# Row DFT by sums and differences of the half rows, and z1 units moved into the row-DFT stage

## The chip, the cores and the metric

The kernel runs on one core of a Trainium2 chip. The metric is the device time of one execution in microseconds. Before the change the median of three runs is 530.57 us (530.54 to 532.73). The core has TensorE (PE; its weight loads are shown apart as PEld), VectorE (DVE), ScalarE (ACT), GpSimd (POOL) and SyncE (SP, which here only issues DMAs).

## The reference

The input x has 2048 rows of 576 numbers in bfloat16. Its rows are normalised, and the result goes two ways: through a spectral filter (a two-dimensional real FFT, a product with complex weights, and back), and through a gated network whose second half is mixed over the rows by a 2048 x 2048 matrix.

```
xn  = layernorm(x)                                  # rows of 576
s   = irfft2(rfft2(xn) * (A_w_r + 1j*A_w_i))        # 2048 x 289 frequencies
z   = gelu(xn @ B_w_in)                             # 576 -> 4608
z1  = z[:, :2304];  z2 = layernorm(z[:, 2304:])
g   = B_w_sp @ z2 + B_b_sp                          # mixes the 2048 rows
out = x + s * silu((z1 * g) @ B_w_out)
```

## The kernel before

The row index is cut into 16 tiles of 128 rows, the 576 columns into four blocks of 128 and a tail of 64 (`KS` = 5 blocks, the last filled up with zeros). Transforms are matrix products with constant matrices. The stages, with the times at which TensorE is in them:

- **Row DFT** (13.64 to 39.59 us, after a start with warm-up matmuls and the first two tiles). For each tile m: `ln1` makes mean and variance on DVE (L234, L235) and 1/sqrt on POOL (L223, L225, a power); for the first two tiles ACT and DVE do it. `xpose` normalises on DVE (L250), transposes the five blocks on TensorE (L254), and ACT copies the result to `xnT` (L255), which stays on chip for everything that follows. `p0` multiplies the five blocks by the cosine and sine columns (L263, ten matmuls of 289 columns), ACT evicts both results (L266), and POOL issues the DMA that writes them to `Ad` in DRAM (L267).
- **Column DFT** p1 (L281, from 51.61), p2 with the filter's weights and p3 (78.03 to 132.85), **inverse** p4 and p5 (L331, L346; 132.85 to 175.66). Between them the data go through DRAM (`Ad`, `Bd`, `Ed`), and p5 writes s to `Yd` (L354).
- **Units of z2 and z1**, which fill the waits of the stages above. A z2 unit (`z2`, 96 of them) is one row tile by 384 columns: five matmuls (L370), a gelu on ACT (L374 or L380) into `Z2`, which stays on chip; sums for its normalisation are made by ACT for seven of the tiles (L377) and by DVE for the others, and a finished row tile is normalised in place on DVE. A z1 unit (`z1`, 72 of them) is 128 columns of z1 by 512 rows: five matmuls (L434) and a gelu (L437) into one of two buffers of 128 x 2048; after the fourth unit of a column tile ACT's queue writes the buffer to `Z1d` in DRAM (L439), 18 writes of 512 KB. w_in for z1 comes in groups of three column tiles (`load_win1`, two buffers).
- **Slabs.** After p5, SP issues twelve transposing DMAs of w_sp (`load_slabs`, L415). `fill(32)` and a last `fill` put what is left of z2 and z1 beside them, `slab_sums` prepares sums of the slabs on DVE.
- **Main products** (228.87 to the end at 529.2): w_sp times z2 in a scheme of seven products (`main`, L480), and the output product (`outm`, L524).

`fill(n, kinds=...)` takes the next n units; "2" means z2, "1" z1, "21" by turns; where one kind has run out, the other is taken. The order on SP, PE and DVE is the order of the program's text; on ACT and POOL the framework's scheduler sets it. All PSUM tiles of transposes, z1 and z2 come from one pool of four buffers (`psh`), those of p0 to p5 from a pool of two (`psa`). DMAs that SP and ACT issue are given one of eight completion semaphores in turn, in the order of the schedule; a DMA waits, on its issuing engine, for the DMA that held that semaphore before, and instructions behind it on that engine wait with it.

The order of the row-DFT stage is written by hand:

```
for m in range(2, MT):
    if m + 2 < MT:
        ln1([m + 2])
    if m + 1 < MT:
        xpose(m + 1)
    p0(m)
    if m >= 9:
        fill(1, norm=False)
```

Of the kernel before, what the change touches and what calls it, by code (L numbers as in the profile page):

```python
# [26 lines left out]

def build_consts(S, D, L, LC0):
    tp = 2.0 * np.pi
    KS = (D + P - 1) // P  # L30
    d = np.arange(KS * P)[:, None]
    l = np.arange(L)[None, :]
    ang = tp * ((d * l) % D) / D
    cd = np.stack([np.cos(ang), -np.sin(ang)], axis=1)
    cd[D:] = 0.0
    cd = cd.reshape(KS, P, 2 * L).transpose(1, 0, 2).reshape(P, KS * 2 * L)

    s1 = np.arange(N1)
    k1 = np.arange(N1)
    lo, hi = k1 // N2, k1 % N2  # L40
    pos = [4 * hi + 2 * c + lo for c in range(2)]
    g1 = np.zeros((N2, P, P))
    g4 = np.zeros((N2, P, P))
    for s2 in range(N2):
        th = -tp * (((s1[:, None] * k1[None, :]) % N1) / N1 + s2 * k1[None, :] / S)
        co, si = np.cos(th), np.sin(th)
        for c, c2, v in ((0, 0, co), (1, 0, -si), (0, 1, si), (1, 1, co)):
            g1[s2, c * N1 + s1[:, None], pos[c2][None, :]] = v
        cot, sit = co.T, -si.T
        for c, c2, v in ((0, 0, cot), (1, 0, -sit), (0, 1, sit), (1, 1, cot)):  # L50
            g4[s2, pos[c][:, None], c2 * N1 + s1[None, :]] = v
    m2 = np.zeros((P, P))
    m3 = np.zeros((P, P))
    a = np.arange(N2)
    th = -tp * ((a[:, None] * a[None, :]) % N2) / N2
    co, si = np.cos(th), np.sin(th)
    for lo_ in range(2):
        for c, c2, v in ((0, 0, co), (1, 0, -si), (0, 1, si), (1, 1, co)):
            m2[c * N1 + lo_ * N2 + a[:, None], c2 * N1 + 2 * a[None, :] + lo_] = v
        for c, c2, v in ((0, 0, co), (1, 0, si), (0, 1, -si), (1, 1, co)):  # L60
            m3[c * N1 + 2 * a[:, None] + lo_, c2 * N1 + lo_ * N2 + a[None, :]] = v
    m3j = np.concatenate([m3[N1:], -m3[:N1]], axis=0)
    mm = np.stack([m2, m3, m3j], axis=1).reshape(P, 3 * P)

    ceso = np.zeros((P, len(LC0), 2, L))
    dd = np.arange(L)[None, :]
    seen = 0
    for i, l0 in enumerate(LC0):
        lv = (l0 + np.arange(P))[:, None]
        th = tp * ((lv * dd) % D) / D  # L70
        cl = np.where((lv == 0) | (lv == D // 2), 1.0, 2.0) * (lv >= seen) * 0.5 / (S * D)
        ceso[:, i, 0, :] = cl * np.cos(th)
        ceso[:, i, 1, :] = -cl * np.sin(th)
        seen = l0 + P
    return dict(cdsd=cd, g1=g1.transpose(1, 0, 2).reshape(P, N2 * P), g4=g4.transpose(1, 0, 2).reshape(P, N2 * P),
                mm=mm, ceso=ceso.reshape(P, -1))
# [3 lines left out]
def kernel(  # L80
# [64 lines left out]
    nc.gpsimd.memset(mhalf[:], -0.5)  # L145

    sizes = dict(A0=12288, G4=N2 * P, CESO=NLC * 2 * L, MM=3 * P, STG=6 * L, TT=8 * L,
                 AIN=4 * 8 * L, BES=2 * 8 * L, RW=KS * Fh, XT=MT * KS * P, XN=2048, ZT=2048, WI=2 * KS * WG * P)
    offs, o_ = {}, 0
    for k_, v_ in sizes.items():  # L150
        offs[k_] = o_
# [3 lines left out]
    def reg(name, off, n):  # L155
        return AR[:, offs[name] + off: offs[name] + off + n]

    CDSD = reg("A0", 0, KS * 2 * L).rearrange("p (k c l) -> p k c l", k=KS, c=2)
    G1 = reg("A0", KS * 2 * L, N2 * P).rearrange("p (s k) -> p s k", s=N2)
    wo = KS * 2 * L + N2 * P  # L160
    WCH = [reg("A0", wo + i * 8 * L, 8 * L).rearrange("p (c h l) -> p c h l", c=2, h=4) for i in range(2)]
# [3 lines left out]
    MM = reg("MM", 0, 3 * P).rearrange("p (a k) -> p a k", a=3)  # L165
    XN = [reg("XN", i * KS * P, KS * P) for i in range(3)]
    STG = [reg("STG", i * 2 * L, 2 * L) for i in range(3)]
    PST = [reg("BES", i * 2 * L, 2 * L) for i in range(8)]
    AIN = [reg("AIN", i * 8 * L, 8 * L) for i in range(4)]
    TT = [reg("TT", i * 4 * L, 4 * L).rearrange("p (c h l) -> p c h l", c=2, h=2) for i in range(2)]  # L170
    BES = [reg("BES", i * 8 * L, 8 * L) for i in range(2)]
    WIN1 = [reg("WI", i * KS * WG * P, KS * WG * P).rearrange("p (k f) -> p k f", k=KS) for i in range(2)]
    WIN2 = reg("RW", 0, KS * Fh).rearrange("p (k f) -> p k f", k=KS)
    xnT = reg("XT", 0, MT * KS * P).rearrange("p (m k t) -> p m k t", m=MT, k=KS)
    Z1S = [reg(n_, 0, S) for n_ in ("XN", "ZT")]

    SL = reg("A0", 0, 7 * HM * NT).rearrange("p (b s t) -> p b s t", b=7, s=HM)
    ro = [offs["AIN"]]
# [21 lines left out]
    def load_x(c):  # L200
        t = AIN[c][:, 0:4 * D].rearrange("p (m d) -> p m d", m=4)
        if c == 0:
            for i in range(4):
                nc.sync.dma_start(out=t[:, i, :], in_=xv[:, i, :])
                if i == 0:
                    nc.sync.dma_start(out=CDSD, in_=cd_cdsd.ap().rearrange("p (k c l) -> p k c l", k=KS, c=2))
        else:
            nc.sync.dma_start(out=t, in_=xv[:, 4 * c:4 * c + 4, :])
        return t

    wv = B_w_in[0:(KS - 1) * P, :].rearrange("(k p) f -> p k f", p=P)
    XC = [load_x(c) for c in range(4)]
    nc.gpsimd.memset(WIN2[KT:P, KS - 1, :], 0.0)
    for g in range(2):
        sl = slice(g * Fh // 2, (g + 1) * Fh // 2)
        gl = slice(Fh + g * Fh // 2, Fh + (g + 1) * Fh // 2)
        nc.sync.dma_start(out=WIN2[:, 0:KS - 1, sl], in_=wv[:, :, gl])
        nc.sync.dma_start(out=WIN2[0:KT, KS - 1, sl], in_=B_w_in[(KS - 1) * P:D, gl])
    nc.sync.dma_start(out=G1, in_=cd_g1.ap().rearrange("p (s k) -> p s k", s=N2))

    def rstd_of(mv, n, tag):
# [25 lines left out]
    def xpose(m):  # L247
        xn = XN[m % 3]
        mean, rs = ln1_of[m]
        nc.vector.tensor_scalar(out=xn[:, 0:D], in0=XC[m // 4][:, m % 4, :], scalar1=mean, scalar2=rs,  # L250
                                op0=ALU.subtract, op1=ALU.mult)
        pt = psh.tile([P, KS, P], BF16, tag="h")
        for ks in range(KS):
            nc.tensor.transpose(pt[:, ks, :], xn[:, ks * P:(ks + 1) * P], ident[:])  # L254
        nc.scalar.activation(out=xnT[:, m, :, :], in_=pt[:], func=ACT.Identity)  # L255

    Adw = Ad[:].rearrange("(c m p) l -> m p c l", c=2, p=P)

    def p0(m):
        pa = psa.tile([P, 2, 512], F32, tag="a")  # L260
        for ks in range(KS):
            for c in range(2):
                nc.tensor.matmul(pa[:, c, 0:L], lhsT=xnT[:, m, ks, :], rhs=CDSD[:, ks, c, :],  # L263
                                 start=(ks == 0), stop=(ks == KS - 1))
        sg = PST[m % 8].rearrange("p (c l) -> p c l", c=2)
        nc.scalar.activation(out=sg, in_=pa[:, :, 0:L], func=ACT.Identity)  # L266
        nc.gpsimd.dma_start(out=Adw[m], in_=sg)  # L267

    rowv = lambda t: t[:].rearrange("(p s) l -> p (s l)", s=N2)
    colv = lambda t: t[:].rearrange("(h p) l -> p h l", p=P)  # L270
# [155 lines left out]

    SA = dict(P1=0, P2=1, P5=2, P4=3, P6=4, P7=5, P3=6)

    def z1(k):
        fi, tq = k // 4, k % 4  # L430
        wb = WIN1[(fi // WG) % 2]
        ph = psh.tile([P, 512], F32, tag="h")
        for ks in range(KS):
            nc.tensor.matmul(ph[:].rearrange("p (a t) -> p a t", a=4), lhsT=wb[:, ks, (fi % WG) * P:(fi % WG + 1) * P],  # L434
                             rhs=xnT[:, 4 * tq:4 * tq + 4, ks, :], start=(ks == 0), stop=(ks == KS - 1))
        zs = Z1S[fi % 2]
        nc.scalar.activation(out=zs[:, tq * 512:(tq + 1) * 512], in_=ph[:], func=ACT.Gelu_apprx_tanh)  # L437
        if tq == 3:
            nc.scalar.dma_start(out=Z1d[fi * P:(fi + 1) * P, :], in_=zs)  # L439
            if fi % WG == WG - 1 and fi // WG + 2 < FT // WG:  # L440
                load_win1(fi // WG + 2)

    Z1v = Z1d[:].rearrange("(f p) (h t) -> p f h t", p=P, h=2)

# [89 lines left out]
    def it_of(m):  # L534
        return (m % HM) * P // NT

    def load_win1(g):
        fs = slice((g % (FT // WG)) * WG * P, (g % (FT // WG) + 1) * WG * P)
        wb = WIN1[g % 2]
        nc.sync.dma_start(out=wb[:, 0:KS - 1, :], in_=wv[:, :, fs])  # L540
        nc.sync.dma_start(out=wb[0:KT, KS - 1, :], in_=B_w_in[(KS - 1) * P:D, fs])

    units = [(it, p) for it in range(len(ITS)) for p in range(NP)]
    zq = iter(range(MT * NZC))
    yq = iter(range(FT * 4))
# [21 lines left out]
    with tc.manual_schedule(engines={SP, PE, DVE}):  # L567
# [4 lines left out]
        ln1([0])  # L572
        xpose(0)
        nc.sync.dma_start(out=MM, in_=cd_mm.ap().rearrange("p (a k) -> p a k", a=3))
        p0(0)
        ln1([1])
        xpose(1)
        ln1([2])
        p0(1)
        ln1([3])  # L580
        xpose(2)
        for m in range(2, MT):
            if m + 2 < MT:
                ln1([m + 2])
            if m + 1 < MT:
                xpose(m + 1)
            p0(m)
            if m == 2:
                nc.scalar.activation(out=scr[:], in_=ln1_of[3][0], func=ACT.Gelu_apprx_tanh)
            if m >= 9:  # L590
                fill(1, norm=False)
    with tc.manual_schedule(engines={SP, PE, DVE}):
        for ch in range(4):
            p1_read(ch)
        load_w(0)
        load_w(1)
        for i in range(2):
            nc.gpsimd.memset(WIN1[i][KT:P, KS - 1, :], 0.0)
            load_win1(i)
        fill(14)  # L600
        for s2 in range(0, N2, 2):
            p1(s2)
# [12 lines left out]
            p3(hh)  # L615
        for ch in range(4):
            p4_read(ch)
        fill(12, kinds="21")
        for u in range(4 * NLC):
            p4(u)  # L620
            fill(1, kinds="21"[u % 2])
        for j in range(MT):
            p5(j)
            fill(1, kinds="21"[j % 2])
        load_slabs(0)
        fill(32, kinds="21")
        assert z2_done[0] == MT * NZC - 1
        nc.sync.dma_start(out=BB, in_=B_b_sp.rearrange("(a s) -> a s", a=1).to_broadcast((P, S)))
        load_z1(0)
# [53 lines left out]
```

## Time and profile before

The profiled execution took 530.98 us, of which the profile's span covers 529.2.

| stage | from, to (us) | length | PE busy | DVE | ACT | POOL | DMA share |
|---|---|---|---|---|---|---|---|
| start, warm-up | 0 to 13.64 | 13.64 | 8.57 | 7.55 | 6.78 | 6.46 | 0.90 |
| row DFT | to 39.59 | 25.95 | 25.95 | 14.66 | 21.62 | 18.19 | 0.58 |
| 14 z2 units | to 51.61 | 12.02 | 12.02 | 5.66 | 10.47 | 3.45 | 0.60 |
| p1 and units | to 78.03 | 26.42 | 24.12 | 20.21 | 22.84 | 4.13 | 0.67 |
| p2, p3 and units | to 132.85 | 54.82 | 54.15 | 34.07 | 37.40 | 4.87 | 0.82 |
| p4, p5 and units | to 175.66 | 42.81 | 42.81 | 24.95 | 29.51 | 2.06 | 0.42 |
| slab loads, units | to 228.87 | 53.21 | 52.28 | 23.32 | 28.19 | 7.07 | 0.85 |
| main products, output | to 529.20 | 300.33 | 291.03 | 215.13 | 23.67 | 125.58 | 0.32 |

How to read the profile's lines: a line of the groups names source line, engine, operation, output and inputs by the program's names (AR is the one large buffer that most tiles are parts of, ph, pa, pb and pm are PSUM), the shapes, the count; then busy time and the mean of one in ns; then the idle time of the engine just before them and what ended most of it. A timeline line begins with start and duration. A line of the waits says which instruction waited for which, how long in total, how often, and the longest. A line of stages has from:to, its length, and the busy time and number of instructions of PE, PEld, DVE, ACT and POOL, then granted TensorE clock, DMA share and GB/s.

### The profile page before, as it was taken

The numbers are of one execution on the slowest core, as the hardware profiler recorded it, in microseconds if no ns is written. First come the engines' busy times: TensorE is split into PE (matmuls) and PEld (weight loads), VectorE is DVE, ScalarE is ACT, GpSimd is POOL, SyncE is SP. The second block draws the span as 40 slices with busy tenths as digits, with TensorE's granted clock in tenths as the row PEclk, the third lists the DMA queues.
The fourth block names the chain that finished last, engine by engine and source line by source line (L and its number), as shares of the span: only waits on it lengthen the run. The fifth ranks groups of instructions, "written<-read, shape, count | busy, mean of one in ns | idle before, by whom it ended". The sixth has DMA issues, their size and how long they took to land.

```text
span 529.2 us, 9153 instructions
## 1 busy us (share of the span) xinstructions
PE 510.9 (97%) x3516; PEld 335.2 (63%) x3516; DVE 345.6 (65%) x660; ACT 180.5 (34%) x380; POOL 171.8 (32%) x230
## 2 busy tenths in 40 slices
PE   6999899999999999999999999999999999999997
PEld 3876555555666544456666677756666677788775
DVE  5925867863456635437777765986867638899944
ACT  5788887686875555420000001100000011000001
POOL 4852210001000002124434323534444234655510
PEclk9999999999999999999999999999999999999999
DMA  8926769875524799482111199312121942211102
GB/s 316 288 81 227 222 189 332 226 214 186 173 80 131 172 192 243 181 301 70 31 55 36 44 185 202 96 37 60 31 59 31 152 129 88 65 33 38 42 6 86
DMA packets 80444, 70.50 MB, mean 133 GB/s; under 512 B 38288, under 2 KB 70800, under 8 KB 80144
## 3 DMA queue, kind: packets, MB, share of 16 engines
q1 hardware_dynamic: 74784, 51.59, 37.7%
q0 software_dynamic: 2880, 8.86, 5.7%
q10 hardware_dynamic: 2736, 9.47, 4.8%
q8 instruction: 27, 0.44, 0.4%
q14 instruction: 17, 0.14, 0.1%
HBM read 40.25 MB, written 21.26 MB: 116 GB/s over the span
## 4 chain that ended last, share of the span: by engine, by line
PE 75%; DVE 9%; DMA 6%; issue 5%; ACT 2%; SPq 2%; POOL 1%; DVEq 0%; ACTq 0%; POOLq 0%
PE pm L480 33%; PE po L524 11%; PE ph L434 10%; PE ph L370 10%; DVE AR L484 4%; PE pa L263 3%; DMA AR<-in_B_w_sp_dram 3%; PE pa L346 2%; DVE AR L489 2%; SPq L415 2%; PE pb L317 2%; DMA Z1d<-AR 1%; DMA AR<-Bd 1%; PE pa L331 1%; DMA AR<-in_A_x_dram 1%
## 5 line engine op out<-in xcount | busy, mean ns | idle before, releaser
L480 PE MATMUL pm<-AR,Z_74 128*128 128x384 bf16 (+1 forms) x864 | 138.7, 308 | 0.0
L484 DVE TENSOR_TENSOR AR<-pm,AR 128x384 f32<-128x384 f32 (+3 forms) x162 | 82.3, 508 | 58.0 <-POOL AR L493 33.3
L480 PE MATMUL pm<-AR 128*128 128x384 bf16 (+1 forms) x648 | 107.0, 308 | 5.5 <-DVE AR L484 5.5
L480 PEld LDWEIGHTS <-Z_74 128*128 128x128 bf16 x864 | 84.5, 98 | 40.6
L370 PE MATMUL ph<-AR 128*128 128x384 bf16 x480 | 90.1, 326 | 0.5 <-ACT Z_74 L380 0.5
L480 PEld LDWEIGHTS <-AR 128*128 128x128 bf16 x648 | 63.3, 98 | 37.4 <-DVE AR L466 4.0
L434 PE MATMUL ph<-AR 128*128 128x512 bf16 x360 | 86.2, 379 | 0.5 <-ACT AR L437 0.5
L492 ACT ACTIVATE AR<-pm 128x384 f32<-128x384 f32 (+1 forms) x27 | 12.3, 456 | 191.3 <-PE pm L480 191.3
L468 POOL TENSOR_TENSOR AR<-Z_74,AR 128x1024 bf16<-128x1024 bf16 x27 | 57.7, 2139 | 43.0 <-PE pm L480 32.9
L524 PE MATMUL po<-AR 128*128 128x288 bf16 x540 | 66.6, 286 | 0.0
L524 PEld LDWEIGHTS <-AR 128*128 128x128 bf16 x594 | 56.9, 98 | 13.9
L370 PEld LDWEIGHTS <-AR 128*128 128x128 bf16 x480 | 46.7, 98 | 29.4 <-issue 0.7
L489 DVE TENSOR_TENSOR AR<-AR 128x384 bf16<-128x384 bf16 (+1 forms) x108 | 57.9, 536 | 3.7
L434 PEld LDWEIGHTS <-AR 128*128 128x128 bf16 x360 | 34.9, 98 | 35.2 <-issue 0.8
L437 ACT ACTIVATE AR<-ph 128x512 bf16<-128x512 f32 x72 | 42.3, 596 | 35.6 <-PE ph L434 31.4
L493 POOL TENSOR_TENSOR AR<-AR 128x384 f32<-128x384 f32 (+1 forms) x27 | 23.6, 873 | 88.9 <-ACT AR L492 88.9
L223 POOL TENSOR_SCALAR ve<-mv 128x1 f32<-128x1 f32 x30 | 5.8, 195 | 94.6 <-DVE mv L398 86.5
L527 ACT ACTIVATE TH<-po 128x576 f32<-128x576 f32 x15 | 9.8, 651 | 78.5 <-PE po L524 78.5
L380 ACT ACTIVATE Z_74<-ph 128x384 bf16<-128x384 f32 x54 | 26.1, 491 | 14.0 <-PE ph L370 10.5
L528 DVE SCALAR_TENSOR_TENSOR AR<-TH,po 128x576 bf16<-128x576 f32 x15 | 11.3, 752 | 29.9 <-ACT TH L527 29.9
L307 DVE TENSOR_TENSOR AR<-pa,AR 128x578 bf16<-128x578 f32 x32 | 22.8, 754 | 10.7 <-PE pa L305 8.7
L512 POOL DMA_DIRECT2D AR<-Yd x16 | 8.7, 547 | 55.8 <-DVE AR L529 52.7
(98 smaller groups left out, 507.9 us busy)
## 6 DMA issues: line engine op xcount, KB each, us to landing
Z1d<-AR ACTq DMA_DIRECT2D x18, 512.0 KB, 4.4
AR<-Z1d SPq DMA_DIRECT2D x36, 192.0 KB, 3.0
AR<-in_B_w_out_dram SPq DMA_DIRECT2D x1, 2592.0 KB, 11.2
Ad<-AR POOLq DMA_DIRECT2D x16, 144.5 KB, 4.1
AR<-Ad SPq DMA_DIRECT2D x4, 578.0 KB, 5.7
AR<-in_A_w_r_dram SPq DMA_DIRECT2D x16, 144.5 KB, 4.6
AR<-in_A_w_i_dram SPq DMA_DIRECT2D x16, 144.5 KB, 4.0
Bd<-AR SPq DMA_DIRECT2D x4, 578.0 KB, 2.8
```

The source lines that it names most:

```text
L263: nc.tensor.matmul(pa[:, c, 0:L], lhsT=xnT[:, m, ks, :], rhs=CDSD[:, ks, c, :], start=(ks == 0), stop=(ks == KS - 1))
L307: nc.vector.tensor_tensor(out=tt[:, c, :, :], in0=pa[:, :, 0:L], in1=wt[:, c, hh % 4:hh % 4 + 2, :], op=ALU.mult)
L370: nc.tensor.matmul(ph[:], lhsT=xnT[:, m, ks, :], rhs=WIN2[:, ks, n * ZC:(n + 1) * ZC], start=(ks == 0), stop=(ks == KS - 1))
L380: nc.scalar.activation(out=zc, in_=ph[:], func=ACT.Gelu_apprx_tanh)
L434: nc.tensor.matmul(ph[:].rearrange("p (a t) -> p a t", a=4), lhsT=wb[:, ks, (fi % WG) * P:(fi % WG + 1) * P], rhs=xnT[:, 4 * tq:4 * tq + 4 ...
L437: nc.scalar.activation(out=zs[:, tq * 512:(tq + 1) * 512], in_=ph[:], func=ACT.Gelu_apprx_tanh)
L468: nc.gpsimd.tensor_tensor(out=t, in0=zblk(p, 1, 0), in1=t2, op=ALU.subtract)
L480: nc.tensor.matmul(dst, lhsT=z[:, s, :], rhs=SL[:, SA[name], s, 0:nt], start=(s == 0 and not more), stop=(s == HM - 1), skip_group_check=more)
L484: nc.vector.tensor_tensor(out=out, in0=x, in1=y, op=ALU.add)
L489: nc.vector.tensor_tensor(out=o, in0=o, in1=zb[:, f, h, 0:nt], op=ALU.mult)
L493: nc.gpsimd.tensor_tensor(out=p1a, in0=p1, in1=B[0], op=ALU.add)
L524: nc.tensor.matmul(pv[:, hh, :], lhsT=U[:, fi, h, i * P:(i + 1) * P], rhs=WOUT[:, fi, c0 + hh * H2:c0 + hh * H2 + w // nh], start=(fi == 0 ...
```

## The change

The DFT of a row of 576 is split by the parity of the frequency. With a and b the first and the second 288 columns, even frequencies need only a + b and odd ones only a - b, with the same cosine and sine columns. `xpose` now writes the normalised row so that blocks 0 and 1 of the two halves lie by turns (in two instructions, 512 and 64 columns), and the transposed blocks are added and subtracted on DVE by a new `p0_fold`. The tails of the two halves, 32 columns each, share the fifth block, which is not folded. `p0` has six matmuls of 290 columns for ten of 289, the constant is 445 KB for 740, and ACT's eviction puts even and odd frequencies back in order with a stride of two. The rows of w_in are loaded in the same order as the blocks (`load_win`, four DMAs in place of two), and its first group for z1 is loaded ahead of the part for z2.

The order changes too. In the row-DFT loop `ln1([m + 2])` comes after `xpose(m + 1)`. Units fill that loop from m = 3 on, ten of z1 and three of z2 (before: seven of z2 from m = 9 on). The units beside p4 and p5 are z2 alone (before: by turns), and after p5 only z1 is left. z1 units go by group, then by quarter of the rows, then by column tile; each writes its own 128 KB (72 writes), from four buffers for the first sixteen units and eight after that.

```diff
-    CDSD = reg("A0", 0, KS * 2 * L).rearrange("p (k c l) -> p k c l", k=KS, c=2)
+    LE = L - L // 2
+    CDSD = reg("A0", 0, 12 * LE).rearrange("p (a k l) -> p a k l", a=2, k=3)
+    FS = [reg("G4", i * 4 * P, 4 * P).rearrange("p (a b t) -> p a b t", a=2, b=2) for i in range(4)]
...
-    Z1S = [reg(n_, 0, S) for n_ in ("XN", "ZT")]
+    Z1S = [reg("ZT", i * 512, 512) for i in range(4)]
...
+    wv = [B_w_in[a * H2:a * H2 + 2 * P, :].rearrange("(b p) f -> p b f", p=P) for a in range(2)]
+    HT = H2 - 2 * P
+
+    def load_win(t, fs):
+        for a in range(2):
+            nc.sync.dma_start(out=t[:, a:KS - 1:2, :], in_=wv[a][:, :, fs])
+            nc.sync.dma_start(out=t[a * HT:(a + 1) * HT, KS - 1, :], in_=B_w_in[a * H2 + 2 * P:(a + 1) * H2, fs])
...
+    load_win1(0)
...
-        nc.sync.dma_start(out=WIN2[:, 0:KS - 1, sl], in_=wv[:, :, gl])
-        nc.sync.dma_start(out=WIN2[0:KT, KS - 1, sl], in_=B_w_in[(KS - 1) * P:D, gl])
+        load_win(WIN2[:, :, sl], gl)
+    load_win1(1)
...
-        nc.vector.tensor_scalar(out=xn[:, 0:D], in0=XC[m // 4][:, m % 4, :], scalar1=mean, scalar2=rs,
+        xr = XC[m // 4][:, m % 4, :].rearrange("p (a d) -> p a d", a=2)
+        nc.vector.tensor_scalar(out=xn[:, 0:4 * P].rearrange("p (b a i) -> p a b i", b=2, a=2),
+                                in0=xr[:, :, 0:2 * P].rearrange("p a (b i) -> p a b i", b=2), scalar1=mean, scalar2=rs,
                                 op0=ALU.subtract, op1=ALU.mult)
+        nc.vector.tensor_scalar(out=xn[:, 4 * P:D].rearrange("p (a i) -> p a i", a=2), in0=xr[:, :, 2 * P:H2],
+                                scalar1=mean, scalar2=rs, op0=ALU.subtract, op1=ALU.mult)
...
+    def p0_fold(m):
+        xe, xo = xnT[:, m, 0:KS - 1:2, :], xnT[:, m, 1:KS - 1:2, :]
+        nc.vector.tensor_tensor(out=FS[m % 4][:, 0, :, :], in0=xe, in1=xo, op=ALU.add)
+        nc.vector.tensor_tensor(out=FS[m % 4][:, 1, :, :], in0=xe, in1=xo, op=ALU.subtract)
...
-        for ks in range(KS):
-            for c in range(2):
-                nc.tensor.matmul(pa[:, c, 0:L], lhsT=xnT[:, m, ks, :], rhs=CDSD[:, ks, c, :],
-                                 start=(ks == 0), stop=(ks == KS - 1))
+        for par in range(2):
+            for k in range(3):
+                lhs = FS[m % 4][:, par, k, :] if k < 2 else xnT[:, m, KS - 1, :]
+                nc.tensor.matmul(pa[:, par, 0:2 * LE], lhsT=lhs, rhs=CDSD[:, par, k, :], start=(k == 0), stop=(k == 2))
         sg = PST[m % 8].rearrange("p (c l) -> p c l", c=2)
-        nc.scalar.activation(out=sg, in_=pa[:, :, 0:L], func=ACT.Identity)
-        nc.gpsimd.dma_start(out=Adw[m], in_=sg)
+        nc.scalar.activation(out=sg.rearrange("p c (l a) -> p a c l", a=2),
+                             in_=pa[:, :, 0:2 * LE].rearrange("p a (c l) -> p a c l", c=2), func=ACT.Identity)
+        nc.gpsimd.dma_start(out=Adw[m], in_=sg[:, :, 0:L])
...
+    z1_order = [(WG * g + i, tq) for g in range(FT // WG) for tq in range(4) for i in range(WG)]
...
-        fi, tq = k // 4, k % 4
+        fi, tq = z1_order[k]
...
-        zs = Z1S[fi % 2]
-        nc.scalar.activation(out=zs[:, tq * 512:(tq + 1) * 512], in_=ph[:], func=ACT.Gelu_apprx_tanh)
-        if tq == 3:
-            nc.scalar.dma_start(out=Z1d[fi * P:(fi + 1) * P, :], in_=zs)
-            if fi % WG == WG - 1 and fi // WG + 2 < FT // WG:
-                load_win1(fi // WG + 2)
+        zs = Z1S[k % 4] if k < 16 else Z1L[k % 8]
+        nc.scalar.activation(out=zs, in_=ph[:], func=ACT.Gelu_apprx_tanh)
+        nc.scalar.dma_start(out=Z1d[fi * P:(fi + 1) * P, tq * 512:(tq + 1) * 512], in_=zs)
+        g, r = k // (4 * WG), k % (4 * WG)
+        if r == 4 * WG - 1 and g + 2 < FT // WG:
+            load_win1(g + 2)
+
+    Z1L = Z1S + [reg("XN", i * 512, 512) for i in range(4)]
...
         for m in range(2, MT):
+            p0_fold(m)
+            if m + 1 < MT:
+                xpose(m + 1)
             if m + 2 < MT:
                 ln1([m + 2])
-            if m + 1 < MT:
-                xpose(m + 1)
             p0(m)
...
-            if m >= 9:
-                fill(1, norm=False)
+            if m >= 3:
+                fill(1, norm=False, kinds="2" if m % 4 == 2 else "1")
...
-        for i in range(2):
-            nc.gpsimd.memset(WIN1[i][KT:P, KS - 1, :], 0.0)
-            load_win1(i)
...
-        fill(12, kinds="21")
+        fill(12)
         for u in range(4 * NLC):
             p4(u)
-            fill(1, kinds="21"[u % 2])
+            fill(1)
         for j in range(MT):
             p5(j)
-            fill(1, kinds="21"[j % 2])
+            fill(1)
         load_slabs(0)
-        fill(32, kinds="21")
+        fill(32, kinds="1")
```

## The prediction

> **What bounds the kernel now.** I read the busy shares first, then the same shares by stage (the span cut where TensorE passes from one stage to the next), then the timeline of one row-DFT tile, then the chain and the waits of the stretch before the main products. All times are of the profiled execution: 530.98 us, 0.41 us above the 530.57 median; its span is 529.2.
>
> ```profile
> PE 510.9 (97%) x3516; PEld 335.2 (63%) x3516; DVE 345.6 (65%) x660; ACT 180.5 (34%) x380; POOL 171.8 (32%) x230
> 13.64:39.59 25.95, 25.95 (x235) 20.10 (x232) 14.66 (x46) 21.62 (x43) 18.19 (x36) 1.00 0.58 181
> 132.85:175.66 42.81, 42.81 (x329) 28.03 (x328) 24.95 (x49) 29.51 (x60) 2.06 (x7) 1.00 0.42 123
> 175.66:228.87 53.21, 52.28 (x261) 25.31 (x260) 23.32 (x40) 28.19 (x52) 7.07 (x11) 1.00 0.85 201
> L370 PE MATMUL ph<-AR 128*128 128x384 bf16 x480 | 90.1, 326 | 0.5 <-ACT Z_74 L380 0.5
> L434 PE MATMUL ph<-AR 128*128 128x512 bf16 x360 | 86.2, 379 | 0.5 <-ACT AR L437 0.5
> ```
>
> The last three numbers of a stage are granted TensorE clock (1.00 throughout), DMA share and GB/s. TensorE is busy for the whole row-DFT stage (13.64 to 39.59), so work removed there is worth its full time only if nothing else has that same 26 us to do: ACT already has 21.6, POOL 18.2. Between the inverse DFT and the main products (175.66 to 228.87) TensorE is also full, on z1 and z2 units alone, at a DMA share of 0.85. At the stage rates a z2 unit costs 0.81 us of TensorE and a z1 unit 1.08 (the rows' means are longer because matmuls overlap).
>
> One tile of the row DFT:
>
> ```profile
> 21.10 0.21 DVE L235 BATCH_NORM_AGGREGATE mv<-st 128x2 f32<-128x12 f32 x1
> 21.30 1.42 PE L263 MATMUL pa<-AR 128*128 128x289 bf16 x10
> 21.54 0.43 DVE L250 TENSOR_SCALAR AR<-AR,mv,rs 128x576 bf16<-128x576 bf16 x1 [0.23 <-POOL rs L225]
> 21.59 0.19 POOL L223 TENSOR_SCALAR ve<-mv 128x1 f32<-128x1 f32 x1
> 21.77 0.70 ACT L255 ACTIVATE AR<-pt 128x640 bf16<-128x640 bf16 x1
> 21.86 0.55 POOL L225 TENSOR_TENSOR rs<-ve,mhalf 128x1 f32<-128x1 f32 x1
> 21.88 0.81 DVE L234 BATCH_NORM_STATS2 st<-AR 128x6 f32<-128x288 bf16 x2
> 22.76 0.65 ACT L266 ACTIVATE AR<-pa 128x578 bf16<-128x578 f32 x1 [0.29 <-PE pa L263]
> ```
>
> Tiles pass every 1.53 us. The statistics of a tile (L234, L235) are made one normalisation ahead, so the power on POOL (L225) is ready about when L250 wants it: the wait is only 0.23.
>
> Last, the loads of w_sp, their waits and the chain:
>
> ```profile
> DMA to landing us min/median/max: 4.0/4.9/8.8
> ACT AR L437 <- DMA Z1d<-AR: 3.5, 1, 3.5
> ACT Z_74 L380 <- DMA AR<-in_B_w_sp_dram: 3.1, 1, 3.1
> 187.73 7.40 DMA AR<-in_B_w_sp_dram
> 195.20 0.33 ACTq L439 DMA_DIRECT2D Z1d<-AR  x1
> 200.15 8.82 DMA AR<-in_B_w_sp_dram
> 209.05 6.14 DMA Z1d<-AR
> ```
>
> ACT stands still behind transposing loads that it never reads. The landing of the sixth load (195.12) lets a z1 write go at 195.20, that of the twelfth (208.97) one at 209.05. SP's and ACT's DMAs share eight completion semaphores in turn, and a DMA waits, on the engine that issues it, for the one that held its semaphore before. TensorE lost only 1 us, because one write follows every fourth z1 unit, and the four PSUM buffers reach over about 4 us.
>
> **A. Row-DFT stage.** Removed: per tile 10 matmuls of 289 columns, replaced by 6 of 290. Ten take 1.25 us in the chain, so 4 x 0.125 x 16 tiles = 8.0 us of TensorE. Added per tile on DVE: two 128x256 additions; the same operation takes 232 ns at 144 columns and 307 at 288 (L529), so 0.29 each, 0.58 in all. L250 is split in two: 0.43 becomes about 0.50. The eviction L266 writes with a stride: 0.65 if that is free, up to 1.0 by L338 (1.02, a rearranging eviction of 1024 columns). One z1 unit or z2 unit per tile comes in from tile 3 on.
>
> The order changes too. Statistics of tile m+2 stood ahead of the normalisation of m+1; now they stand behind it. Two loops through DVE follow, each one tile long:
> - normalise 0.40 to the mean's first use, statistics 0.84 + 0.21, semaphore 0.15, L223 0.20 + 0.09, L225 0.56, 0.03: about 2.5 us;
> - normalise 0.50, transposes 0.54, eviction L255 0.75, additions 0.63: about 2.4 us.
> ACT has 0.70 + 0.65 + 0.60 (gelu) + 0.33 (write) and gaps, about 2.45; TensorE only 0.28 + 0.75 + 1.08 = 2.11. So tiles pass every 2.5 us (bounds: 2.1 if only TensorE counts, 2.85 if the strided eviction takes 1.0 and ACT bounds). The third normalisation starts at about 11.75, 0.17 later than now (its power sits behind a POOL DMA issue). The last starts at 11.75 + 13 x 2.5 = 44.25; transposes, eviction, additions, the last six matmuls and a z1 unit bring 48.6; 14 z2 units (11.4) bring the column DFT to 60.0 instead of 51.61: +8.4. Ten z1 units ran here that came later, and four z2 units fewer: 10.8 - 3.25 = 7.55. Net +0.85: the 8.0 saved are spent waiting.
>
> **B. Column DFTs, weights, inverse** (p1 to p5; 124.05 us now, TensorE full). 19 z1 units give way to 19 z2 units: 19 x 0.27 = -5.1. In p2/p3, 16 z1 writes stand where 4 did, each with 0.33 of issue and a semaphore that an SP load may hold; queued behind each on ACT are a gelu and the eviction that feeds p3. Nothing shows such a wait there now: bounds 0 and +5 (the 3.1 and 3.5 us waits above, less what PSUM hides), I take +2, nearest to one such wait with half hidden. More z2 normalisations under p4 and p5 (DVE 25 of 43 us): +0.5. One DVE wait of 1.3 us in p1 may ease: -0.6. B gives -3.2, so p5 ends 5.2 later. The quicker constant load (740 to 445 KB) and w_in in four transfers instead of two lie under 3 us of DVE waiting for x at the start: 0, at most 1 us either way.
>
> **C. Before the main products** (53.2 us now). Only z1 units are left: 46 (49.7 us of TensorE; now 37 z1 and 15 z2, 52.2). Each z1 unit now ends in a 128 KB write, so in the order in which semaphores are given out in the changed program z1 writes 31 to 38 wait for the landings of loads 1, 2, 3, 5, 6, 7, 8, 10, and write 40 for load 12. Unit 27 is the first after p5, one unit takes 1.08 us: write 31 comes up after 4.5 us, its load lands at about 7; from there on ACT goes at the loads' pace. The first load is issued about 3.0 us after p5 (4.4 now; the pair of w_in loads ahead of it is gone, 1.45). The twelfth lands 28.9 us after that now; I take 27.5. Bounds: 24.4, the 12 x 1.7 us that their packets held all sixteen DMA engines (20.4) plus the shortest landing of 4.0; and 31, two more than now, since loads 6, 7 and 9 to 12 in turn wait for the landings of z1 writes 28 to 33. So write 40 goes at 30.5. ACT then evicts unit 41 (0.33 + 0.60), which frees a PSUM buffer at 31.5; units 45 to 72 remain, 28 x 1.08 = 30.3; two waits for w_in 0.5. Main starts at 62.3 instead of 53.2: **+9.1**. The main products are not touched.
>
> **Sum**: 0.85 + 7.55 - 3.2 + 9.1 = +14.3, or 545 us.
>
> The smaller writes themselves I cost at nothing: a write of 512 KB now lands 4.4 us after its issue (median), no later instruction of ACT wants its result within that time but the gelu that reuses its buffer, four to eight units (4.3 to 8.7 us) on, and a quarter of the bytes should not land later. [...] No row here shows that a write's latency reaches TensorE where its semaphore is free, so the sum is left without it.
>
> **Rivals.**
> 1. *The row-DFT loops are shorter than their rows* (2.1 us a tile, TensorE's own need): -5.5, 539 to 540. For: the additions may run beside POOL. Against: the second loop has no POOL in it and still needs 2.4.
> 2. *p2/p3 or the loops stall more*: +5 instead of +2, or 2.85 us a tile (+4.9): 548 to 553.
> 3. *Not slower: the loads of w_sp do not hold ACT.* Place: z1 units 31 to 44. If the twelfth load lands early, C is TensorE's 49.7 and the total 545.3 - 12.6 = 532.7. It decides if main can start 50.5 us after p5, that is, load 12 landed 15.7 us after the first issue. Against: 28.9 now, and 20.4 us of packets.
> 4. *The change does what its words say*: eight us saved, z1 units merely moved: 523. That needs loop and loads both to be hidden.
>
> **How the numbers follow.** Forecast (541 to 549) 0.60; rival 1, 0.13; rival 2, 0.16; rival 3, 0.07; rival 4, 0.04. From the forecast, loads at the lower bound take 3.1 and a loop of 2.4 takes 1.4: 541; with rival 1 also 536. Upwards rival 2 with one cause reaches 550, with load 12 at 31 us 553. Leaving out 3 and 4 and the tail of 2: 536 to 552. Half a per cent (2.7 us) is what a measurement of this kernel tells from no change. Rival 4 is faster, 0.04; rival 3 same, 0.06; the rest slower, 0.90.
>
> **What would show it.** 96 matmuls in p0; normalisations 2.5 us apart, with DVE waiting for POOL's power or for ACT; 72 writes to Z1d of 128 KB; p1 starting near 60; about 12 us of TensorE idle after p5, its waits on the gelu, and gelus waiting on the w_sp loads; main starting near 243 instead of 229. If normalisations come every 2.1 us, A was wrong; if TensorE is full before main, C was, and with it the sign.

## The result, and the profile after

The changed kernel takes 549.97 us (547.97 to 550.63), the kernel before 531.65 in the runs that belong to it (530.54 to 535.61): 1.0324 times as long, with an interval of 1.0262 to 1.0387. The forecast was 545, range 536 to 552. The profiled execution took 549.94 us.

By the places where TensorE passes from one step of the prediction to the next (first matmuls of p1, last of p5, first of the main products):

| step | before, us | after, us | change | predicted |
|---|---|---|---|---|
| A: start to column DFT | 51.6 | 62.1 | +10.5 | +8.4 |
| B: column DFT to end of p5 | 124.1 | 124.8 | +0.7 | -3.2 |
| C: end of p5 to main products | 53.2 | 59.7 | +6.5 | +9.1 |
| main products, output | 300.3 | 301.2 | +0.9 | 0 |

Of the +10.5 of A, 7.55 are units moved into this stage (the prediction's count); B and C have as much less to do.

A line of the changed kernel's page (its span is 547.8 us), and two of its stages: row DFT, and p5 to the main products, 0.3 us cut off at its start (length; busy time of PE, PEld, DVE, ACT, POOL; granted TensorE clock, DMA share, GB/s):

```profile
PE 511.8 (93%) x3452; PEld 329.6 (60%) x3452; DVE 355.0 (65%) x708; ACT 184.0 (34%) x380; POOL 173.2 (32%) x230
...
13.64:51.10 37.46, 32.01 (x222) 18.14 (x220) 26.39 (x90) 30.68 (x49) 21.65 (x41) 0.96 0.67 191
...
187.20:246.45 59.25, 52.89 (x229) 22.71 (x228) 11.90 (x19) 26.17 (x45) 4.43 (x5) 0.94 0.81 204
```

64 matmuls fewer, and TensorE is not less busy: 511.8 us instead of 510.9. Part of its work was done at a lower clock (0.96 and 0.94 in these two stages, 1.00 in both before), and in both it now waits. One tile of the row DFT, from the timeline (start, length):

```profile
21.35 0.21 DVE L263 BATCH_NORM_AGGREGATE mv<-st 128x2 f32<-128x12 f32 x1
...
21.92 0.67 POOL L253 TENSOR_TENSOR rs<-ve,mhalf 128x1 f32<-128x1 f32 x1
...
22.63 0.41 DVE L279 TENSOR_SCALAR AR<-AR,mv,rs 128x512 bf16<-128x512 bf16 x1 [0.27 <-POOL rs L253]
...
25.30 0.41 DVE L279 TENSOR_SCALAR AR<-AR,mv,rs 128x512 bf16<-128x512 bf16 x1 [0.46 <-POOL rs L253]
```

From one normalisation (22.63) to the next (25.30) are 2.67 us, 2.5 were predicted, 1.53 is what it was before. Eleven of the last thirteen wait for the power on POOL, which starts when the statistics made just before are there. That is the first loop of the prediction. The longest waits of TensorE up to the main products, and that of ACT for loads of w_sp:

```profile
PE pt L286 <- DVE AR L279: 10.3, 14, 3.2
PE ph L474 <- ACT AR L477: 6.1, 6, 2.0
PE pb L355 <- DVE AR L345: 3.2, 3, 1.8
PE pa L319 <- DVE AR L323: 2.5, 2, 1.7
```

```profile
ACT AR L477 <- DMA AR<-in_B_w_sp_dram: 11.3, 7, 3.4
```

And the chain inside the stretch after p5 (start, length):

```profile
201.07 4.60 DMA AR<-in_B_w_sp_dram
...
205.75 0.34 ACTq L478
...
206.13 0.61 ACT AR L477
...
211.95 3.93 DMA AR<-in_B_w_in_dram
```

A load of w_sp lands at 205.67, a z1 write is issued at 205.75, and the next gelu follows at 206.13. The trace's list of transfers has the same step, 0.07 to 0.08 us from landing to issue, for nine of the ten writes 31 to 40 (write 39 follows 38 at its own pace), in the pairs that the prediction named (the DMAs of SP and ACT in this trace name eight completion semaphores between them, and each of the nine writes names that of its load): write 31 goes after load 1, 32 after 2, 33 after 3, 34 after 5, and so on to write 40 at 213.21, after load 12 landed at 213.14. The last line is a load of w_in for the next group of z1 units, which SP could only issue behind the twelve loads; more of it below.

### The profile page after: what moved, and what is told of

Its sections match the earlier page's. It is cut to its first block, busy times and chain, and to the rows that moved or that the text cites. A ratio compares the mean times of both kernels' runs of the same rounds, so it can differ in the third digit from the quotient of the medians.

```text
span 547.8 us, 9217 instructions
## 1 busy us (share of the span) xinstructions
PE 511.8 (93%) x3452; PEld 329.6 (60%) x3452; DVE 355.0 (65%) x708; ACT 184.0 (34%) x380; POOL 173.2 (32%) x230
## 4 chain that ended last, share of the span: by engine, by line
PE 62%; DVE 14%; ACT 6%; issue 6%; DMA 5%; POOL 4%; SPq 1%; ACTq 0%; DVEq 0%; POOLq 0%
PE pm L522 32%; PE po L566 10%; PE ph L474 8%; PE ph L408 5%; DVE AR L526 4%; DMA Z1d<-AR 3%; POOL rs L253 2%; PE pa L384 2%; ACT Z_74 L412 2%; ACT TH L415 2%; DVE AR L531 2%; DVE st L262 1%; PE pb L355 1%; ACT AR L477 1%; DVE Z_74 L447 1%
## 5 line engine op out<-in xcount | busy, mean ns | idle before, releaser
L526 DVE TENSOR_TENSOR AR<-pm,AR 128x384 f32<-128x384 f32 (+3 forms) x162 | 82.3, 508 | 74.1 <-POOL AR L535 49.7
L408 PE MATMUL ph<-AR 128*128 128x384 bf16 x480 | 88.4, 326 | 0.0
L510 POOL TENSOR_TENSOR AR<-Z_74,AR 128x1024 bf16<-128x1024 bf16 x27 | 57.8, 2139 | 58.3 <-PE pm L522 32.7
L463 DVE TENSOR_TENSOR AR<-AR 128x1024 bf16<-128x1024 bf16 x32 | 21.9, 690 | 19.4 <-DMA AR<-in_B_w_sp_dram 18.6
L345 DVE TENSOR_TENSOR AR<-pa,AR 128x578 bf16<-128x578 f32 x32 | 22.8, 751 | 12.5 <-PE pa L343 5.1
L570 DVE SCALAR_TENSOR_TENSOR AR<-TH,po 128x576 bf16<-128x576 f32 x15 | 11.3, 753 | 29.9 <-ACT TH L569 29.9
```

The lines of the kernel that those rows point to most:

```text
L345: nc.vector.tensor_tensor(out=tt[:, c, :, :], in0=pa[:, :, 0:L], in1=wt[:, c, hh % 4:hh % 4 + 2, :], op=ALU.mult)
L408: nc.tensor.matmul(ph[:], lhsT=xnT[:, m, ks, :], rhs=WIN2[:, ks, n * ZC:(n + 1) * ZC], start=(ks == 0), stop=(ks == KS - 1))
L463: nc.vector.tensor_tensor(out=SL[:, o, :, sl], in0=SL[:, a, :, sl], in1=SL[:, b, :, sl], op=op)
L510: nc.gpsimd.tensor_tensor(out=t, in0=zblk(p, 1, 0), in1=t2, op=ALU.subtract)
L526: nc.vector.tensor_tensor(out=out, in0=x, in1=y, op=ALU.add)
```

## Experiments

Two things had to be told apart for A: whether the place of the statistics or the additional work sets the pace. For C, whether it is the writes on ACT that starve TensorE, or the loads themselves. All edits are to the changed kernel unless said otherwise.

### The statistics a tile ahead again

```diff
-            p0_fold(m)
-            if m + 1 < MT:
-                xpose(m + 1)
             if m + 2 < MT:
                 ln1([m + 2])
+            p0_fold(m)
+            if m + 1 < MT:
+                xpose(m + 1)
```

> The changed kernel, with the statistics of tile m+2 back ahead of the normalisation of tile m+1 in the row-DFT loop; nothing else. Theory (the lost lookahead: DVE waits for POOL's power once a tile): the loop through POOL is gone, what is left is normalise 0.70, transposes and eviction 1.05 to 1.3, additions 0.6, so 2.35 to 2.5 us a tile instead of the 2.67 measured; last normalisation near 43 to 44.5 instead of 46.6, total 545.5 to 548. Rival (the pace is set by ACT or by DVE's own work, the power is late only because all is): tiles stay at 2.6 to 2.7, total within 1 us of the changed kernel.

545.37 us (544.40 to 548.41), 4.6 below the changed kernel and at the edge of what was expected; the last normalisation is at 42.1, p1 starts at 57.6 instead of 62.1. The timeline of two tiles, then DVE's only wait of the stage:

```profile
26.40 0.41 DVE L279 TENSOR_SCALAR AR<-AR,mv,rs 128x512 bf16<-128x512 bf16 x1
...
28.74 0.41 DVE L279 TENSOR_SCALAR AR<-AR,mv,rs 128x512 bf16<-128x512 bf16 x1
```

```profile
DVE AR L293 <- ACT AR L287: 4.5, 8, 1.3
```

No wait for POOL is left, and a tile takes 2.34 us. What holds it now is the second loop: normalise, transpose, evict, add. So the lost lookahead cost 4 to 5 us. What is left of A, 6.0 us (57.6 against 51.6), is less than the 7.55 us of units that now run here: by this estimate some 1.5 of the 8.0 us of matmuls come through while the second loop sets the pace.

### The fold alone

The kernel before with sums and differences only; statistics ahead, additions behind the next normalisation, units, writes and loads' order as before:

```diff
 for m in range(2, MT):
     if m + 2 < MT:
         ln1([m + 2])
     if m + 1 < MT:
         xpose(m + 1)
+    p0_fold(m)
     p0(m)            # six matmuls
     if m >= 9:
         fill(1, norm=False)
```

> The kernel before with the sums and differences alone: six matmuls, two additions, split normalisation, strided eviction; units, writes, loads and the statistics' order as before, additions behind the next normalisation. Theory (the fold moves the bound of a tile from TensorE to DVE): DVE needs 0.58 + 0.70 + 1.02 = 2.3 us a tile against TensorE's 1.03 without a unit, so tiles 2 to 8 pass at 2.3 instead of 1.53 and tiles 9 to 15 at 2.3 to 2.4 as now: about +5.5, 535 to 538. Rival (the matmuls saved come through): -5 to -8, 523 to 526.

534.85 us (533.02 to 538.68) against 531.41, 1.0068 times (1.0039 to 1.0097): the eight us of matmuls taken out of TensorE make the kernel 3.4 us slower, less than the 5.5 expected. The timeline of one tile without a unit:

```profile
20.92 0.28 DVE L289 TENSOR_TENSOR AR<-AR 128x256 bf16<-128x256 bf16 x1
...
21.32 0.81 DVE L258 BATCH_NORM_STATS2 st<-AR 128x6 f32<-128x288 bf16 x2
...
22.29 0.37 DVE L275 TENSOR_SCALAR AR<-AR,mv,rs 128x512 bf16<-128x512 bf16 x1
...
22.79 0.28 DVE L289 TENSOR_TENSOR AR<-AR 128x256 bf16<-128x256 bf16 x1
```

DVE works without a gap, and the next additions begin 1.87 us after the last ones. Back to back its instructions overlap a little (its two additions take 0.28 each and start 0.20 apart), so a tile costs 1.87 instead of the sum of 2.3. Before, a tile without a unit took 1.53. DVE has become the bound of the stage.

### z1 writes off ACT

```diff
-        nc.scalar.dma_start(out=Z1d[...], in_=zs)
+        (nc.gpsimd if k >= 26 else nc.scalar).dma_start(out=Z1d[...], in_=zs)
```

> The changed kernel, with the z1 writes from unit 26 on (after p5) issued by POOL instead of ACT, so that they share no semaphores with the w_sp loads and block no gelu. Theory (writes held by the w_sp loads hold ACT): no gelu waits on a w_sp load, TensorE is full after p5, main starts 50 to 53 us after p5 instead of 59.6, total 541 to 544. Rival (TensorE starves there for another reason, the clock or DMA load): still 58 us or more, total within 1.5 us of the changed kernel.

550.49 us (547.65 to 550.78): no gain, although the cause that the theory names is gone. From the timeline after p5, SP's loads and the first of TensorE's matmuls behind its wait:

```profile
189.69 24.10 SPq L453 DMA_TRANSPOSE AR<-in_B_w_sp_dram  x12
213.90 0.52 SPq L229 DMA_DIRECT2D AR<-in_B_w_in_dram  x1
...
217.32 0.61 PE L474 MATMUL ph<-AR 128*128 128x512 bf16 x1 [7.49 <-DMA AR<-in_B_w_in_dram]
```

No gelu waits on a load of w_sp any more, and TensorE is full to 209.8. There the 49th unit begins a new group (group 4), and their part of w_in is still to be loaded: SP may load it as soon as the 36th unit has been computed, but has the twelve loads of w_sp ahead of it until 213.8. The prediction has only "two waits for w_in 0.5" for these loads; it followed what the loads of w_sp hold on ACT, not what stands behind them on SP.

The writes beside p2 and p3 moved to POOL as well (`k >= 10`):

> As the run before, but all z1 writes from unit 10 on go by POOL, so those beside p2 and p3 too. Theory (in p1 to p5 the writes' semaphores delay the weight loads that DVE waits for): 2 to 4 us below the run with only the late writes on POOL. Rival (TensorE's extra idle time in p1 to p5 is DVE's: more z2 normalisations and late weights whatever the writes do): equal to it within 1 us.

547.54 us (545.01 to 549.82), 2.9 below the run before in the median, with overlapping spreads. In its trace B takes 122.6 us, in that of the run before 124.0, in that of the changed kernel 124.8; TensorE waits 1.7, 1.5 and 3.2 us for L345. The last two programs have the same writes in B, so 0.8 us is what two executions differ by; with three of the runs that follow and the one with the statistics ahead, six executions with these writes take 124.0 to 125.1. The writes' part in B is then 1.4 to 2.5 us, from one execution without them. Most of what separates this trace from that of the run before lies in C (57.0 us against 61.3), which the edit does not touch. What all of them share is DVE: 2.5 us of waits at L323.

### The loads of w_sp cut in two

```diff
-        load_slabs(0)
-        fill(32, kinds="1")
+        load_slabs(0, (0, 2))
+        fill(9, kinds="1")
+        load_slabs(0, (1, 3))
+        fill(23, kinds="1")
```

Alone, with writes on ACT:

> The changed kernel with the w_sp loads cut in two as in the run before, the z1 writes on ACT as they were. Theory (two covers of like length: the writes held on ACT, and the w_in load behind the w_sp loads; taking one leaves the other): gelus still wait on w_sp loads for 6 us or more, main starts 56 to 61 us after p5's end, total 546 to 551. Rival (the queue place of the w_in load alone is the cause): main 53 us or less after p5, total 543.5 or less.

548.54 us (546.28 to 551.06), main 56.4 us after p5, and gelus wait 7.4 us on loads of w_sp: one of the two covers off, the other still there. With the late writes on POOL as well:

> The changed kernel with the late z1 writes (unit 26 on) on POOL and, besides, the twelve w_sp loads cut in two: six right after p5, six after nine more z1 units, so that the w_in load for z1 group 4 goes between them and that for group 5 behind them instead of both behind all twelve. Theory (with the writes off ACT the next wait is the w_in load queued on SP behind the w_sp loads: 7.5 us in the run with POOL writes): TensorE is full after p5, main starts 50 to 53 us after p5's end, total 540 to 543.5. Rival (what starves it is the DMA load of that stretch as such): still 57 us or more, total 547 or more.

549.98 us (548.07 to 551.17), again no gain, and neither theory nor rival as it was put: TensorE is full from p5 to 223.3, although the DMA share is 0.86 and, from 200 to 215, 1.16, so it is not the DMA load; then one wait of 7.3 us comes. ACT waits 10.3 us for z1 writes to land there. TensorE's waits after p5, and POOL's timeline:

```profile
PE ph L474 <- ACT AR L477: 7.3, 1, 7.3
```

```profile
225.15 2.62 POOL L510 TENSOR_TENSOR AR<-Z,AR 128x1024 bf16<-128x1024 bf16 x1 [13.29 <-DVE AR L506]
227.72 6.98 POOL L478 DMA_DIRECT2D Z1d<-AR  x13
```

The scheduler had put the first operand sum of the main products (L510) on POOL ahead of z1 writes. It waited 13.3 us for a sum on DVE that stands behind the last slab sums, the writes stood behind it, and the gelus ran out of their eight buffers. With that one sum on DVE:

```diff
-            nc.gpsimd.tensor_tensor(out=t, in0=zblk(p, 1, 0), in1=t2, op=ALU.subtract)
+            (nc.vector if u == 0 else nc.gpsimd).tensor_tensor(out=t, in0=zblk(p, 1, 0), in1=t2, op=ALU.subtract)
```

> The run with the late z1 writes on POOL and the w_sp loads cut in two, and besides the first operand sum of the main products (1024 columns) on DVE instead of POOL, where the scheduler had put it ahead of z1 writes and where it waited for the last w_sp load (ten us of gelus waiting for their buffers). Theory (no wait of the stretch is left, and each of the runs before only met the next one in line): TensorE is full from p5 to the main products, which start 50 to 52 us after p5's end instead of 59.6; total 540.5 to 543. Rival (time will not come down whatever is freed, since the loads and the sums of slabs that main needs end late): 57 us or more, total 547 to 551.

539.97 us (539.76 to 541.04), 10.0 below the changed kernel. Of four stretches from p5 to main (186.5 to 236.6) the only one in which TensorE is not busy throughout, and their sum:

```profile
215.00:230.00 15.00, 14.49 (x68) 6.41 (x67) 9.33 (x14) 8.04 (x14) 7.12 (x14) 1.00 0.96 280
...
sum 50.10, PE 49.59 PEld 22.31 DVE 12.87 ACT 27.22 POOL 26.07; mean PE 12.40 PEld 5.58 DVE 3.22 ACT 6.80 POOL 6.52
```

TensorE is busy for 49.59 of 50.1 us, at full clock, and main starts 50.2 us after p5; the wait that is left, 0.5 us, is for w_in. The 46 units need 46 x 1.08 = 49.7. So the loss in C was queues alone. Two are in the changed kernel, each long enough to hide most of the other: writes behind loads on ACT's semaphores, and a load behind loads on SP. The third, writes behind a sum on POOL, came only with the writes on POOL and hid the gain again.

### z1 and z2 by turns again

```diff
             p4(u)
-            fill(1)
+            fill(1, kinds="21"[u % 2])
...
             p5(j)
-            fill(1)
+            fill(1, kinds="21"[j % 2])
         load_slabs(0)
-        fill(32, kinds="1")
+        fill(32, kinds="21")
```

> The changed kernel with z1 and z2 units by turns beside p4, beside p5 and after p5, as in the kernel before (13 z2 units are then left after p5, and a write follows every second unit); writes still 128 KB on ACT. Theory (what binds after p5 is how many z1 writes stand in the order of semaphores beside the w_sp loads, and group 4 of w_in is now loaded ahead of them): the waits on w_sp loads shrink but do not go, main starts 51 to 56 us after p5's end, and the time given back beside p4 and p5 (14 units by 0.27 us) comes out of that: total 543 to 548. Rival (the mixture does not matter): 549 to 551.

544.10 us (542.85 to 547.22), 5.9 below the changed kernel. Gelus still wait for loads of w_sp:

```profile
ACT Z L418 <- DMA AR<-in_B_w_sp_dram: 10.2, 4, 3.7
```

But main starts 50.9 us after p5 and TensorE waits only 4.1 us there: with fewer writes in the row of semaphores the same blocking is mostly covered. Of the 8.9 us by which C is shorter, some 3.5 are work (13 z2 units stand there for z1 units, 0.27 us each), which B has to do instead.

### Can the fold be made to pay?

Three attempts from the kernel with the fold alone. First, z2 units from tile 4 on and the short second normalisation (64 columns) on POOL:

```diff
-        nc.vector.tensor_scalar(out=xn[:, 4 * P:D]...
+        nc.gpsimd.tensor_scalar(out=xn[:, 4 * P:D]...
...
-            if m >= 9:
+            if m >= 4:
                 fill(1, norm=False)
```

> The kernel before with the sums and differences alone, the additions behind the next normalisation, the short second part of the normalisation (64 columns) on POOL instead of DVE, and z2 units in the row-DFT stage from tile 4 on instead of tile 9. Theory (the fold pays only if DVE is kept below TensorE's need and units take up TensorE's time): DVE needs 1.75 us a tile, TensorE 1.85 with a unit, tiles pass at 1.85 to 2.0, five more units are done there; 524 to 529. [...]

541.60 us (540.28 to 542.91), slower than the 524 to 529 expected and than the fold alone (534.85). From POOL's timeline for one tile (between them lie a DMA issue of 0.81 and an addition of 0.18):

```profile
22.56 0.83 POOL L278 TENSOR_SCALAR AR<-AR,mv,rs 128x64 bf16<-128x64 bf16 x1
...
24.51 0.57 POOL L249 TENSOR_TENSOR rs<-ve,mhalf 128x1 f32<-128x1 f32 x1
```

64 columns that take DVE 0.29 us take POOL 0.83, and they stand ahead of the power in its queue: 2.63 us a tile. TensorE also waits 2.4 us there for w_in.

Second, all on DVE, z2 units from tile 5 on:

> The kernel before with the fold alone, all of the normalisation on DVE, z2 units in the row-DFT stage from tile 5 on instead of tile 9. Theory (DVE sets 2.0 us a tile, 0.2 more than TensorE needs with a unit, so four units of 0.81 fit into time that the fold alone left idle): 3 us below the fold alone (534.85), 530.5 to 533, about the kernel before. Rival (units push the tiles apart one for one): 534 to 536.

541.45 us (537.46 to 544.14). The tiles do pass every 1.87 us with a unit each, as expected, but only up to the fourth unit. There TensorE waits 3.0 us for w_in. SP's waits, up to 60 us:

```profile
SPq L229 <- DMA AR<-in_B_w_in_dram: 14.7, 3, 6.9
```

The split load of w_in writes every second block of a tile (L229), and each of these DMAs is issued only when the one before has landed, 0.01 to 0.02 us after it: it looks as if the framework took the interleaved destinations for overlapping, and the waits are gone in the run below that loads regions that lie apart. The changed kernel has that too (10.6 us of such waits on SP in the first 45 us), where nothing needed the data so early.

The rest of the 6.6 us over the fold alone is explained only in part. By the two traces the column DFT starts 4.6 us later, B is 1.2 longer, and C has the same length although the units moved ahead leave TensorE 2.9 us less to do there: it waits 3.2 us for gelus in C, where the fold alone waits for nothing. Why ACT is late there was not tried.

A variant in which the halves lie column by column, normalised by one instruction with a stride of two:

> As the run before, but the two halves of the normalised row lie column by column in turn, written by one instruction with a stride of two, and the transposes read every second column; the short second part of the normalisation goes. Theory (DVE's occupancy per tile sets the pace): the two parts take 0.53 us of DVE now and one of 576 columns took 0.34 unstrided, so up to 0.19 us a tile less where tiles are bound by DVE, 1 to 3 us below the run before: 528 to 531. Rival (the strided write is slow on DVE, 0.6 us or more): 532 to 536.

588.29 us (586.19 to 591.58). It tells little of the stride: the tail rows of w_in then go to every second partition, the first normalisation waited for the last of these loads (30.3 us, to 35.0), and everything shifted. Its normalisation took 0.61 us, as its rival had it, against 0.41 and 0.29.

Last, loads into regions that lie apart, and 1/sqrt of tiles 2 and 3 on ACT:

```diff
+    wv = B_w_in.rearrange("(a r) f -> r a f", a=2)
...
+        for b in range(2):
+            nc.sync.dma_start(out=t[:, 2 * b:2 * b + 2, :], in_=wv[b * P:(b + 1) * P, :, fs])
...
-        if ms[0] < 2:
+        if ms[0] < 4:
```

> The kernel before with the fold, additions behind the next normalisation, z2 units from tile 5 on, and two more edits: w_in goes by pairs of blocks into regions that lie apart (the interleaved destinations of the split load made each load wait for the landing of the one before: the second half of w_in landed near 30 us instead of 21.7, and a unit waited 3.0 us for it), and 1/sqrt of tiles 2 and 3 by ACT and DVE as for tiles 0 and 1 instead of POOL (2.9 us of DVE waiting for the power of tile 2). Theory (with those two waits gone, DVE's pace of 1.87 us a tile is what is left of the row-DFT stage, and four more units are done in it): third normalisation near 10.5 instead of 13, last one near 35 to 37, column DFT from about 50 with 11 units done, total 526 to 530, below the kernel before. Rival (the fold's time is lost again in a wait that these runs have not met): 531.5 or more.

536.50 us (535.41 to 540.87) against 531.47, the rival's side. The loads land at 21 us, but DVE now waits 3.2 us for the power of tile 4, the first that POOL makes, behind a DMA issue in its queue that waits for ACT's eviction; and TensorE's granted clock is 0.78 from 13.64 to 37.00 (0.50 up to 23.8). No version with the fold beat the kernel before. The statistics put ahead and the cure of C were not run together; if their gains add, that is 549.97 - 4.6 - 10.0 = 535.4, an estimate, and still slower.

## Why the prediction came out as it did

The sign, the two places and their mechanisms were right, and the total is 5 us short of the measured one. That it is no further off is in part luck: in the traces A, B and the main products came out 2.1, 3.9 and 0.9 us longer than their terms, C 2.6 shorter. By its steps:

- **A, the loop through POOL.** Right in mechanism: tiles wait for the power, and with the lookahead restored they do not. The term was mis-sized, 2.5 us a tile for 2.67: 13 x 0.17 = 2.2, the whole difference between +8.4 and +10.5. Statistics to power took longer than the rows, above all L253, 0.68 in the median for 0.56.
- **A, the second loop.** Predicted 2.4, measured 2.34 where it alone binds. That is why the restored order gives 4.6 us and not the whole eight. Rival 1 (2.1 us a tile) fell with it. The additions at 0.29 each were right (0.30 and 0.28 in the median), the strided eviction took 0.82, between the two bounds, and did not bind. The split of L250 was put at 0.50 together; the parts take 0.41 and 0.29, 0.53 as DVE passes through them.
- **B.** The moved units were nearly right (PE busy 116.8 us in the stage, 121.1 before: -4.3, predicted -5.1), the waits were not: TensorE idles 8 us here where it did 3, and +2, +0.5 and -0.6 stood for that. The step that failed is DVE's: I took a p1 wait to ease that grew from 1.3 to 2.5, those at p3 (L345) went from 0.7 to 3.2, and p4 has one of 1.3 where there was none. The two waits of the kernel before:

```profile
PE pa L281 <- DVE AR L285: 1.3, 1, 1.3
PE pb L317 <- DVE AR L307: 0.7, 1, 0.7
```

  That is 5.0 more, all of it TensorE behind DVE. What makes DVE late there (z2 normalisations, or weights that load late: it waits 5.4 us for them, 2.0 before) was not taken apart; the writes account for some 2 us, by one execution, and the cause of the rest stays open.
- **C, the order of semaphores.** Right pair by pair. (By the pace of the four writes before it, write 31 would come up some 6 us after p5 and not 4.5; its load lands at 7.0, as predicted, so nothing hangs on that.) Three sizes were off and partly cancel: the first load is issued 3.6 us after p5 (3.0), the twelfth lands 22.6 us after that (27.5, and below the bound of 24.4, so that was none; that held writes left the loads more room is a guess), and from there to main it takes 33.5 (31.8), with a second stop on a z1 write (0.9 us of TensorE) and half-clock matmuls. That makes +6.5 for +9.1. TensorE idles 6.4 us there where the prediction's signs name about 12.
- **C, what waits next.** This the prediction missed. It named one cover; there were two of like length, and taking the named one away brought nothing until the other was gone, and with it a third that the cure itself had made. Rival 3 asked for load 12 within 15.7 us; in the run with all covers off it landed 32.2 us after the first issue, later than in any, and main still started at 50.2, because nothing that TensorE needed early stood behind it.
- **Writes of 128 KB.** The prediction set a cost of nothing against their size. They land 3.4 us after issue in the median (512 KB: 4.4), and with 46 of them on POOL after p5 TensorE is busy for 49.59 of 50.1 us. Their size cost nothing that these runs show; their number on an engine that also evicts did (gelus wait 11.3 us for loads of w_sp in the changed kernel, 3.1 in the one before).
- **Main products**, +0.9, were put at 0. 0.7 of it arises within their first 100 matmuls, where TensorE waits 0.5 us for a sum on DVE (L526), as it does not in the kernel before. Why that sum is late was not tried.

## What to carry to other kernels

A saving on a full engine is worth what the next engine in the same loop allows: write down each engine's occupancy per tile, with the added work, before counting the matmuls saved; here DVE went to 1.87 us a tile against TensorE's 1.03. In a stage of in-order queues look for every instruction that stands behind the slow transfers and is needed, on each queue and by each shared semaphore, since removing the one that ends last may only uncover another of the same length (here 6.1 us of TensorE behind gelus that waited for loads of w_sp, then 7.5 behind a load of w_in). And a cure that gives no gain does not refute the cause: look at what TensorE waits for then.

## What the runs showed of the hardware

Three times in the changed kernel TensorE's granted clock fell to 0.50, each time after 3.4 us in which TensorE was busy for only 1.20 to 1.46 us, twice without a wait of more than 2.0 us, and matmuls of 512 columns took up to 634 ns there for a median of 379. The changed kernel at its start and after p5, cut where the granted clock (third number from the end) changes:

```profile
6.40:9.80 3.40, 1.20 (x11) 0.78 (x11) 2.50 (x10) 1.90 (x4) 0.26 (x1) 1.00 1.07 381
9.80:12.46 2.66, 0.00 (x1) 0.01 (x1) 0.48 (x3) 0.36 (x1) 1.46 (x2) 0.50 1.11 345
...
197.55:200.95 3.40, 1.36 (x6) 0.48 (x5) 0.03 (x1) 1.03 (x2) 0.00 (x0) 1.00 1.22 267
200.95:204.35 3.40, 2.92 (x7) 0.94 (x7) 0.67 (x1) 0.76 (x2) 0.00 (x0) 0.50 1.22 222
```

The longest wait at the start, 3.2 us for the third normalisation, lasts from 9.3 to 12.46, but the clock is at 0.50 from 9.8 on, when that wait is 0.5 us old, and stays there until 16.6: in the 3.4 us before 9.8 TensorE was busy for 1.20. After p5 no single wait is longer than 2.0 us, and yet the clock is 0.50 for 3.4 us twice, from 200.95 and from 211.2, after 1.36 and 1.46 us of work in the 3.4 us before. With 1.58 us of work, from 108.8 to 112.2, it stays at 1.00. The 46 units keep TensorE busy for 53.4 us instead of 49.6, and 5.6 of that run at half the clock: an estimated 3 us of C. The kernel before has no wait of TensorE over 1.3 us and 1.00 throughout, and so had nothing to price it by. The stretches before these three falls were not idle: TensorE worked for a third of them or more. After the 7.5 us wait of the run with writes on POOL the clock is 0.50 for another 7.4 us, and a matmul of 512 columns took up to 634 ns there for a usual 379.

Short DVE instructions took far more per column in these runs (64 columns 0.29 us, 512 columns 0.41), and POOL took 0.83 for the same 64.
